# A fused attention and long-convolution kernel: both task lists in another sequence, evictions shared anew, and the last spectra's first two PSUM tiles in another pool

## The chip, the cores and the metric

The kernel runs on one core of one Trainium2 chip. The time is device microseconds of one execution, as the median of the runs. Five engines work side by side, each through its own list of instructions in order: PE (TensorE, matmuls; its weight loads are the rows named PEld), DVE (VectorE), ACT (ScalarE), POOL (GpSimd, here almost only DMA issues) and SP (SyncE, DMA issues). An engine waits on a semaphore when its next instruction needs another engine or a DMA, and everything behind that instruction on the same engine waits with it.

## The reference, cut to what matters

`S = L = 2048`, `D = 640`, 32 heads of 20, `N = 192` states. The output mixes a dilated local attention with a long convolution, by a gate per position:

```python
g = sigmoid((x * gate_w).sum(-1, keepdims=True))
# a: 8 keys per query, at distance 0, 2, ..., 14
qkv = x @ wqkv
attn = softmax(where(mask, einsum("bhsd,bhswd->bhsw", q, kg) * scale, -1e9))
a = einsum("bhsw,bhswd->bhsd", attn, vg) ... @ wo
# b: convolution of x with a kernel K made of 192 complex exponentials per channel
P = exp((dt * A)[:, :, None] * l)
K = einsum("dn,dnl,dn->dl", Cc, P, dt * Bc).real
y = irfft(rfft(x padded) * rfft(K padded))[:L] + x * Dskip
out = g * a + (1 - g) * y
```

Both branches read the same `A_x`.

## The kernel before

The work is cut into small tasks. A task has a name, an engine (or, for an eviction from PSUM, either of ACT and DVE), its dependencies, and buffers that it takes and gives back. The strings in `ORDER` hold two lists, `main` (1258 tasks) and `tail` (304): each number is the step to the next task's index in the list of tasks as they were made, and a `D` behind it puts an eviction on DVE, where it would else be ACT's. `Plan.order` reads the string, and `Plan.emit` writes the tasks out in that sequence and ties each instruction to the one before it on its engine. So the string sets the order of every engine, of the DMA queues of SP and POOL among them, and nothing reorders it later. No cost is computed when the kernel is built.

**Projections.** `late{n}` makes tile `n = 15*sc + 5*which + e`: quarter `sc` of the sequence (512 positions), `which` of q, k and v, and head group `e`. It is five matmuls of 128x512 (L281) from `bufA`, which holds the transposed x and `wqkv`, into one of two PSUM tiles named `tb`; `lev{n}` evicts it on ACT or DVE, q and k into the rings `qr` and `kr`, v into `prj`. The loads are issued before the list starts and stand in the same order in both kernels. On SP: `C_re`, `C_im`, the first quarter of x as a DMA transpose (L186), the q block of `wqkv` (L187), `A_im`, `A_re`, the k block, the v block, then quarters 1, 2 and 3 of x.

**Parameters.** Some thirty operations on 128x960 tiles on DVE and ACT (`wr`, `wi`, `tau`, `xl`, `ay`, `at`, and ten pieces `mk0` to `mk9`, tile `pc`) turn the state parameters into ten bf16 pieces, which SP stores (`sp0` to `sp9`, L615) and loads back in another layout (`L0` on SP and POOL, L726, and `L1` to `L9` on SP). On ACT stand among them the logarithm of `xl` (L650), its exponential into `ay` (L654), and `lnd` (L651); DVE's `ay` (L585) needs that exponential.

**Kernel generation.** Ten chunks. In each, `arg` tasks on PE (L761) put arguments into one of two PSUM tiles `ar` of two banks each; ACT takes Sin (L776) and Exp (L778) of them; DVE multiplies them (`pq`, L798 and L800); `kmm` on PE (L816) contracts them into `kps`; `fin` evicts. After chunk 4 half of the kernel is expanded: `near0`, `own0` and `other0`, a store to DRAM (`xst0S` on SP, L892 and L893, and `xst0G` on POOL, L890), and a load back as `kc` (`xld0S`, `xld0G`, L899). `f17` is the first matmul task that reads it (L1264).

**Attention.** Eight blocks of 256 positions: `prod` on DVE (L340), `lg` on PE (L346), the softmax (`max`, `neg`, `exp`, `sum`, `at`), the weights through DRAM on SP (`ast`, `asb`), `pv` on DVE (L409), `gat` on PE (L416), `oT`, the output projection `wo` on PE (L440), its eviction `ga`, and a store by SP (`gaS`, L461). V goes through DRAM on POOL: `lst{sc}2` stores a quarter of `prj` (L310), `vc{position}` loads a window of it (L334). The loads of x for the convolution (`rows`, tile `Usb`, L960) take `prj`'s memory, so the first of them waits for all four stores.

**Transforms.** `f1` and `fk` transform the kernel's two halves, `fu` transforms x; all three use `ar` tiles, and half of the tiles of `fk` use `tb`.

**Tail.** 64 tiles `fp` of four matmuls (L1031), evicted by `sp` tasks on ACT or DVE into spectra; DVE multiplies them (`ta`, `tc`, `Y`); `inv` on PE (L1092), `cp` evictions, `yp` (L1122), scaling and mixing, and the stores of the output. The `fp` tiles take turns in two PSUM pools of two tiles: pool 0 covers the banks that `kps`, `lg` and `tb` had before, pool 1 the banks of the two `ar` tiles. The first tile of a pool waits until the last user of its banks is done.

Of the kernel before, what the change touches and what calls it, by code (L numbers as in the profile page):

```python
# [13 lines left out]
F32 = mybir.dt.float32  # L14
# [26 lines left out]
def _attn_consts():  # L41
# [56 lines left out]
)}  # L98


# [1264 lines left out]
```

## Time and profile before

| | |
|---|---|
| median of 3 runs | 322.88 us (320.05 to 324.29) |
| the profiled execution's own time | 325.58 us |
| its span, first to last instruction | 323.8 us |
| mean granted TensorE clock | 0.966 |
| instructions | 11726 |
| DMA | 45.65 MB in 48697 packets, mean 141 GB/s |
| HBM | 28.25 MB read, 14.01 MB written |

The profiled execution's time is 1.8 us above its span, and 2.7 us above the median of the runs. In a busy line, the first number is microseconds in which the engine worked, then its share of the span and the number of instructions. In a row of the timeline stand the start, the time to the end of the last of the grouped instructions, engine, line, operation, output<-input, how many, and in brackets the idle time just before and what ended it. Neighbouring instructions of one engine overlap a little, so a step from start to start is a better price than a duration.

### The profile page before, as it was taken

Reading aid. Unit: us, or ns where it says so; the run is one execution under the profiler, and the core shown is the slowest. Engines: PE = TensorE matmul, PEld = TensorE weight load, DVE = VectorE, ACT = ScalarE, POOL = GpSimd, SP = SyncE. Lnnn points to the kernel's source line nnn. Section 1 sums busy time; section 2 is a strip of 40 time slices with the busy share of each in tenths; the row PEclk is TensorE's granted clock in tenths of the full one; section 3 lists DMA queues with packets and bytes.
Section 4 is the critical chain, followed back from the end, with each engine's and each line's share of the span. In section 5 each row is a group of like instructions: output and inputs, shape, how many; then the busy total and the mean of one; then the engine's idle time right before and its main releaser. Section 6 shows DMA issues by size and latency. Waiting matters only on the chain.

```text
span 323.8 us, 11726 instructions
## 1 busy us (share of the span) xinstructions
PE 280.7 (87%) x5126; PEld 167.5 (52%) x5126; DVE 289.4 (89%) x395; ACT 281.7 (87%) x422; POOL 55.9 (17%) x87
## 2 busy tenths in 40 slices
PE   0399999999999999999959988888999899997760
PEld 0046544445454555545535454447768676667640
DVE  1999989999999999998967999897998599998882
ACT  1489669999999999999968999799998799997891
POOL 8500073101100000302111302032010000000063
PEclk9999999999999999999998999599999999997995
DMA  8999127943050200558695675544480366873057
GB/s 212 340 221 286 66 61 189 207 116 113 7 124 8 67 5 33 115 103 281 205 237 128 148 167 103 117 134 95 167 304 27 89 211 228 191 146 62 2 134 194
DMA packets 48697, 45.65 MB, mean 141 GB/s; under 512 B 28590, under 2 KB 42482, under 8 KB 48646
## 3 DMA queue, kind: packets, MB, share of 16 engines
q1 hardware_dynamic: 42524, 27.82, 31.8%
q0 software_dynamic: 5216, 16.39, 20.8%
q8 instruction: 40, 0.66, 0.9%
q10 hardware_dynamic: 906, 0.69, 0.7%
q14 instruction: 11, 0.09, 0.1%
HBM read 28.25 MB, written 14.01 MB: 131 GB/s over the span
## 4 chain that ended last, share of the span: by engine, by line
PE 59%; ACT 22%; DVE 7%; DMA 5%; issue 4%; POOL 1%; SPq 0%; DVEq 0%; POOLq 0%; ACTq 0%
PE tb L281 18%; PE ar L761 8%; PE fp L1031 7%; PE tb L440 6%; ACT big L778 6%; PE kps L816 5%; ACT big L776 5%; PE bp L1264 4%; PE tb L416 4%; ACT bufA L468 2%; PE lg L346 2%; DMA bufA<-in_A_x_dram 2%; DMA bufA<-in_A_wqkv_dram 2%; PE cp L1092 2%; ACT bufA L776 2%
## 5 line engine op out<-in xcount | busy, mean ns | idle before, releaser
L281 PE MATMUL tb<-bufA 128*128 128x512 bf16 x300 | 77.3, 393 | 4.6 <-DMA bufA<-in_A_wqkv_dram 4.6
L776 ACT ACTIVATE big<-ar 128x740 bf16<-128x740 int16 (+1 forms) x72 | 56.4, 842 | 5.8 <-PE ar L761 5.5
L761 PE MATMUL ar<-Rarg,L 64*128 64x212 bf16 (+4 forms) x600 | 48.3, 254 | 5.5 <-ACT big L778 2.0
L778 ACT ACTIVATE big<-ar 128x848 bf16<-128x848 f32 x60 | 49.8, 906 | 1.0 <-PE ar L761 0.9
L281 PEld LDWEIGHTS <-bufA 128*128 128x128 bf16 x300 | 31.8, 122 | 35.5 <-issue 9.9
L340 DVE TENSOR_TENSOR prod<-qr,kr 128x2048 bf16<-128x2048 bf16 x40 | 48.0, 1219 | 2.0 <-PE lg L346 2.0
L409 DVE TENSOR_TENSOR pv<-vc,asb 128x2048 bf16<-128x2048 bf16 x40 | 47.5, 1219 | 0.5 <-PE tb L416 0.5
L761 PEld LDWEIGHTS <-L 64*128 64x128 bf16 x600 | 21.1, 95 | 37.5 <-issue 35.6
L798 DVE TENSOR_TENSOR pt<-big 128x1024 bf16<-128x1024 bf16 x48 | 32.7, 702 | 1.5 <-ACT big L776 0.7
L816 PE MATMUL kps<-qq,pt 128*32 128x21 bf16 (+1 forms) x2560 | 28.8, 175 | 5.9 <-issue 5.2
L816 PEld LDWEIGHTS <-pt 128*32 128x32 bf16 (+1 forms) x2560 | 23.5, 92 | 17.6 <-issue 15.4
L440 PE MATMUL tb<-wo_sb,oTm 128*128 128x320 bf16 x160 | 28.5, 315 | 0.1
L334 POOL DMA_DIRECT2D vc<-vS x16 | 11.6, 728 | 85.4 <-DVE pv L409 81.3
L468 ACT ACTIVATE sp_u<-fp 128x640 bf16<-128x640 f32 x30 | 22.5, 886 | 1.4 <-PE fp L1031 1.4
L468 ACT ACTIVATE sp_k<-fp 128x640 bf16<-128x640 f32 x31 | 23.0, 880 | 0.2 <-PE fp L1031 0.2
L416 PE MATMUL tb<-pv,ind 128*64 128x512 bf16 (+1 forms) x192 | 22.2, 350 | 0.2
L800 DVE TENSOR_TENSOR qq<-big 128x1344 bf16<-128x1344 bf16 x24 | 21.2, 885 | 0.0
L1031 PEld LDWEIGHTS <-PHI 128*128 128x128 bf16 x160 | 15.6, 97 | 8.5 <-issue 1.7
L468 ACT ACTIVATE big<-bp 128x1024 bf16<-128x1024 f32 x18 | 18.0, 1043 | 1.3 <-PE bp L1264 1.3
L440 PEld LDWEIGHTS <-oTm 128*128 128x128 bf16 x160 | 14.8, 101 | 8.0 <-issue 3.0
L157 ACT ACT_TABLE_LOAD x14 | 18.0, 1283 | 0.2
L1149 POOL DMA_DIRECT2D out_dram<-ot x14 | 7.8, 561 | 51.2 <-DVE ot L1131 50.4
(149 smaller groups left out, 488.7 us busy)
## 6 DMA issues: line engine op xcount, KB each, us to landing
vc<-vS POOLq DMA_DIRECT2D x16, 327.5 KB, 5.6
vS<-prj POOLq DMA_DIRECT2D x4, 640.0 KB, 5.2
gaS<-ga SPq DMA_DIRECT2D x8, 320.0 KB
Usb<-in_A_x_dram POOLq DMA_DIRECT2D x8, 320.0 KB, 5.0
gaF<-gaS SPq DMA_DIRECT2D x8, 320.0 KB
bufA<-in_A_wqkv_dram SPq DMA_DIRECT2D x3, 800.0 KB
Sprm<-pc SPq DMA_DIRECT2D x10, 240.0 KB
L<-Sprm SPq DMA_DIRECT2D x38, 60.0 KB
```

What stands on the lines that cost most here:

```text
L281: nc.tensor.matmul(ppf, self.wq[:, which, kt, e::5], self.xT[:, c0 // 1024, kt, c0 % 1024:c0 % 1024 + SC], start=(kt == 0), stop=(kt == NK ...
L340: nc.vector.tensor_tensor(b[e][:], self.qr[:, sc % NRB, e, :].unsqueeze(1).to_broadcast([128, W, C]), win(self.kr[:, sc % NRB, e, :], 0, W ...
L409: nc.vector.tensor_tensor(o, vw, b["asb"][:].unsqueeze(2).to_broadcast(sh), ALU.mult)
L416: nc.tensor.matmul(b["op", e][64 * a:64 * a + 64, 0:n, :], ind[:, 32:96], b["pv", e][:, w, a, 0:n, :], start=(w == 0), stop=(w == 3), skip ...
L440: nc.tensor.matmul(apf[:, :320], b["oT"][:, e, i * 128:(i + 1) * 128], wo_sb[:, e, hf * 320:(hf + 1) * 320], start=(e == 0), stop=(e == 4))
L468: nc.scalar.activation(o, i, ACT.Identity)
L761: nc.tensor.matmul(ar[:, g2, a0:a0 + ncol], L[rows, gv, sb, l0:l0 + 128], R[rows, c0:c0 + ncol], start=True, stop=True, tile_position=(64 ...
L776: nc.scalar.activation(d_[:, :, s0 * QW:s1 * QW], ar[:].bitcast(I16)[:, :, 0:2 * (s1 - s0) * QW:2], ACT.Sin, scale=SCL)
L778: nc.scalar.activation(dst[:, gp::2].rearrange("p g s n -> p g (s n)"), ar[:, :, 0:2 * EW], ACT.Exp)
L798: nc.vector.tensor_tensor(pt[:, :, k, :], gg[:, :, ::-1] if k else gg, e1, ALU.mult)
L816: nc.tensor.matmul(kps[32 * g:32 * g + 32, h ^ (g // 2), NM * ql:NM * ql + NM], pt[rows, k, v, :], qq[rows, k, v, :], start=(g not in star ...
L1031: nc.tensor.matmul(fp[:, fl % 2, 0:320].rearrange("p (c x) -> p c x", x=32), phis[fb][:, fl, kind, :], B[:, :, 2 * f1 + ri].rearrange("p c ...
```

## The change

Both strings of `ORDER` are replaced. The tasks, their dependencies and their buffers are the same; the sequence of both lists differs from the first task on, and some evictions change engine. In `main`, ACT evicts 48 of the 60 projection tiles where it evicted 45, 13 of 24 `oT` where it was 17, 21 of 32 `ga` where it was 20, 16 of 20 `fu` where it was 18, 9 of 15 `fk` where it was 8, and 8 of 10 `fin` where it was 6; DVE has the rest. In `tail`, ACT evicts 58 of the 64 `fp` tiles where it was 61, and 12 of the 20 `cp` tiles in both. ACT loads its function tables 14 times in both lists, at the same tasks. The one other edit turns the two pools of the `fp` tiles round:

```diff
 ORDER = {"main": (
-    "55 -48 49 -56 3 -2 3 7 -9 4 2 -3 7 -3 48 -44 -3 13 5 -14 2 -1 7 45 1 1 -17 1 1 -23 -14 8 -1 34 -25 26 1 19 1 1 -34 -29 "
+    "52 1 -52 2 -3 2 5 -1 6 -8 7 -3 46 -41 -8 127 1 1 -119 -6 1 18 -14 65 1 1 -34 -31 1 50 1 1 7 1 1 -23 1 -31 -7 39 13 1 1 "
...
-                    fp = spec[nm, ro, h] = q["ps"][q["nf"] // 2 % 2].tile([128, 2, 512], F32, name="fp")
+                    fp = spec[nm, ro, h] = q["ps"][1 - q["nf"] // 2 % 2].tile([128, 2, 512], F32, name="fp")
```

The first place is the start of PE's list. A row is an instruction with the semaphore that it waits on, the numbers behind a name tell tiles apart, and of the five matmuls of a tile the later ones are left out. Before, the first three projection tiles are `late1`, `late5` and `late0` (q, k and q of quarter 0):

```order
L281 LDWEIGHTS bufA_77 [waits DMAHW7_49]
L281 MATMUL tb_182<-bufA_77 128x512 [waits DMAHW3_49]
...
L281 LDWEIGHTS bufA_77 [waits DMAHW3_49]
L281 MATMUL tb_210<-bufA_77 128x512
...
L281 MATMUL tb_217<-bufA_77 128x512 [waits Activation_49]
```

Now they are `late0`, `late26` (v of quarter 1) and `late9` (k of quarter 0):

```order
L281 LDWEIGHTS bufA_77 [waits DMAHW7_49]
L281 MATMUL tb_182<-bufA_77 128x512 [waits DMAHW3_49]
...
L281 LDWEIGHTS bufA_77 [waits DMAHW4_49]
L281 MATMUL tb_201<-bufA_77 128x512 [waits DMAHW5_49]
...
L281 LDWEIGHTS bufA_77 [waits DMAHW3_49]
L281 MATMUL tb_213<-bufA_77 128x512 [waits Activation_49]
```

What moved: a tile of quarter 1 stands in the second place, and waits for two further loads, the v block of `wqkv` (DMAHW4) and quarter 1 of x (DMAHW5); before, the first tile of quarter 1 was PE's eleventh.

The second place is ACT's list at the same time; `qr`, `kr` and `prj` rows are evictions of those tiles, L650, L651 and L654 are the logarithm, `lnd` and the exponential of the parameters. Before:

```order
L594 ACTIVATE xl_149<-wr_142 128x960
L594 ACTIVATE ax_144<-wr_142 128x960
L594 ACTIVATE xa_148<-wi_143 128x960
L468 ACTIVATE qr_172<-tb_182 128x2x256
L650 ACTIVATE xl_149<-xl_149,bc0_152 128x960
L654 ACTIVATE ay_145<-xl_149 128x960
L651 ACTIVATE lnd_135<-dtb_133 128x5
L468 ACTIVATE kr_173<-tb_210 128x2x256
```

Now:

```order
L594 ACTIVATE xa_148<-wi_143 128x960
L594 ACTIVATE xl_149<-wr_142 128x960
L468 ACTIVATE qr_172<-tb_182 128x2x256
L594 ACTIVATE ax_144<-wr_142 128x960
L468 ACTIVATE prj_181<-tb_201 128x512
L651 ACTIVATE lnd_135<-dtb_133 128x5
L650 ACTIVATE xl_149<-xl_149,bc0_152 128x960
L468 ACTIVATE kr_173<-tb_213 128x2x256
L654 ACTIVATE ay_145<-xl_149 128x960
```

What moved: the evictions of `late26` and `late9` now stand ahead of the logarithm and of the exponential.

The third place is POOL's list around the expanded first half of the kernel (`xst0G` writes `Kx`, `xld0G` reads `kc`). Before, with the stores of quarters 2 and 3 of V (L310) on either side of it (the second reads like the first and is left out):

```order
L310 DMA vS_68<-prj_181 640x1x512
L890 DMA Kx_180<-X_3235 64x4x640
L899 DMA kc_3618<-Kx_180 128x2560
L334 DMA vc_3762<-vS_68 64x10x262 x2
...
L960 DMA Usb_4229<-in_A_x_dram 32x32x160 x2
```

Now, with the store of quarter 3 ahead of these rows, that of quarter 2 among them, and `vc1024` (the last row) behind the first load of `Usb`:

```order
L231 DMA omS_58<-om2_559 16x128
L890 DMA Kx_180<-X_3206 64x4x640
L899 DMA kc_3514<-Kx_180 128x2560
L310 DMA vS_68<-prj_181 640x1x512
L960 DMA Usb_3529<-in_A_x_dram 32x32x160
L334 DMA vc_3918<-vS_68 64x10x262 x2
```

What moved: the store of quarter 2 went from ahead of `xst0G` to behind `xld0G`, and the load of the fifth window of V behind it and behind a load of `Usb` that waits for that store. On SP, `gaS1` now stands ahead of `xst0S`; before, it stood behind it.

82 rows, old and new, of the table ORDER are left out of this document.

## The prediction

> **What bounds the kernel.** I read the page first: busy times, then the shares of the chain that ended last.
>
> ```profile
> span 323.8 us, 11726 instructions
> PE 280.7 (87%) x5126; PEld 167.5 (52%) x5126; DVE 289.4 (89%) x395; ACT 281.7 (87%) x422; POOL 55.9 (17%) x87
> PE 59%; ACT 22%; DVE 7%; DMA 5%; issue 4%; POOL 1%; SPq 0%; DVEq 0%; POOLq 0%; ACTq 0%
> ```
>
> Three engines are at 87 to 89% each, so no one engine is the bound, and a sequence can only win or lose waits. Where waits are left is read from the windows: the time, then busy time and count of PE, PEld, DVE, ACT and POOL, the granted clock, the DMA share and GB/s. The cuts are the first Sin, two spells of stalls, the end of `main` and the last spectra.
>
> ```profile
> 47.40:160.00 112.60, 110.62 (x2393) 56.50 (x2391) 110.09 (x153) 110.17 (x161) 12.50 (x19) 1.00 0.44 113
> 160.00:176.00 16.00, 12.09 (x283) 7.23 (x279) 11.77 (x17) 11.63 (x17) 3.92 (x5) 0.89 0.72 165
> 176.00:200.00 24.00, 21.22 (x571) 12.36 (x572) 23.19 (x30) 23.78 (x35) 6.02 (x8) 1.00 0.59 135
> 200.00:216.00 16.00, 13.35 (x288) 6.72 (x288) 14.28 (x16) 13.69 (x21) 2.83 (x5) 0.79 0.66 145
> 216.00:254.60 38.60, 35.94 (x534) 27.24 (x534) 33.86 (x50) 35.37 (x49) 5.41 (x10) 1.00 0.42 129
> 254.60:293.60 39.00, 36.58 (x258) 24.82 (x259) 35.86 (x51) 36.66 (x61) 0.46 (x2) 1.00 0.74 190
> ```
>
> From the first Sin to 160 us all three are at 98%: nothing lost at the start is made up there. From 160 to the end of `main` ACT idles 4.4 + 0.2 + 2.3 + 3.2 = 10.1 us; that is all that a better sequence could win back.
>
> **The start.** It is the one place where the change adds a wait that rows of before can price. The chain, the DMA packets in two windows (4.9 to 8.1 and 17.2 to 20.1 us), and then PE:
>
> ```profile
> 1.66 7.21 DMA bufA<-in_A_x_dram
> 8.89 6.80 DMA bufA<-in_A_wqkv_dram
> DMA packets 2955, 0.78 MB, mean 242 GB/s; under 512 B 2903, under 2 KB 2955, under 8 KB 2955
> DMA packets 2697, 0.74 MB, mean 256 GB/s; under 512 B 2633, under 2 KB 2697, under 8 KB 2697
> 11.82 2.33 PE L281 MATMUL tb<-bufA 128*128 128x512 bf16 x5 [2.99 <-DMA bufA<-in_A_wqkv_dram]
> 15.74 11.51 PE L281 MATMUL tb<-bufA 128*128 128x512 bf16 x45 [1.59 <-DMA bufA<-in_A_wqkv_dram]
> 17.86 0.15 PEld L281 LDWEIGHTS <-bufA 128*128 128x128 bf16 x1 [0.28 <-issue]
> 18.29 0.84 PEld L281 LDWEIGHTS <-bufA 128*128 128x128 bf16 x4 [0.28 <-issue]
> ```
>
> A quarter of x is 512 x 640 bf16, which is 2560 packets of 256 bytes. Quarter 0 fills the first of the two windows and has landed at 1.66 + 7.21 = 8.87, 0.8 us after the window's end. Quarter 1 fills the second, behind the weight blocks that SP issued ahead of it, so it lands at 20.1 + 0.8 = 20.9 us (20.1 at the earliest). Before, PE's first tile of quarter 1 came eleventh and found it there. Now it is second: PE does `late0` as before from 11.82, and then stands until 20.9 instead of 15.74, 5.2 us more, with `late9` and all that follows queued behind. `late26` takes 5 steps of 0.43 (from 17.86 to 18.29 the clock is still slow) and ends at 23.0.
>
> [...]
>
> What waits for PE at 23.0 are the parameters: ACT now has the evictions of `late26` and `late9` ahead of its logarithm and its exponential.
>
> ```profile
> 16.61 1.10 ACT L650 ACTIVATE xl<-xl,bc 128x960 f32<-128x960 f32 x1 [1.34 <-DVE xl L585]
> 17.74 1.00 ACT L654 ACTIVATE ay<-xl 128x960 f32<-128x960 f32 x1
> 18.65 0.19 ACT L651 ACTIVATE lnd<-dtb 128x5 f32<-128x5 bf16 x1
> 18.75 0.58 ACT L468 ACTIVATE kr<-tb 128x512 bf16<-128x512 f32 x1
> 21.02 1.15 DVE L585 TENSOR_TENSOR ay<-ay,ax 128x960 f32<-128x960 f32 x1
> 22.09 0.65 DVE L606 TENSOR_SCALAR x<-tau 128x960 f32<-128x960 f32 x1
> 22.66 1.15 DVE L585 TENSOR_TENSOR xa<-are,dtb 128x960 f32<-128x960 bf16 x1
> 38.39 1.15 DVE L622 TENSOR_TENSOR pc<-at,t 128x960 bf16<-128x960 f32 x1
> 41.67 0.70 SPq L726 DMA_DIRECT2D L<-Sprm  x2
> 42.18 1.42 POOL L726 DMA_DIRECT2D L<-Sprm  x2 [29.16 <-DMA L<-Sprm]
> L<-Sprm POOLq DMA_DIRECT2D x2, 60.0 KB, 2.6
> 47.00 0.53 PE L761 MATMUL ar<-Rarg,L 64*128 64x296 bf16 x8
> 47.41 2.42 ACT L776 ACTIVATE big<-ar 128x888 bf16<-128x888 int16 x3 [0.18 <-PE ar L761]
> ```
>
> From 23.0: eviction 0.58, `lnd` 0.19, logarithm 1.10, eviction 0.58, exponential 1.00, so 26.5, and only then DVE's `ay`, which stood at 21.02: 5.5 us late. DVE runs its list in order, so nothing covers this: ahead of `ay` the new list has one two-input and one single-input operation fewer, so DVE is there at 21.02 - 1.6 = 19.4 and stands for 7.1 us. Between `ay` and the last parameter piece the new list has one two-input operation (1.07 from 21.02 to 22.09) and one single-input one (0.57 from 22.09 to 22.66) more: 1.6 us. The last piece ends at 39.54 + 5.5 + 1.6 = 46.6 instead of 39.54. From there to `L0` landed it was 42.18 + 1.42 + 2.6 - 39.54 = 6.7 us, so the first `arg` can run at 53.3; it ran at 47.00. PE itself comes there at 47.00 + 5.2 + one more tile (5 steps of about 0.22) = 53.3. **+6.4 us** (bounds: 5.2, PE's pause alone, and 7.1, the delay of the pieces).
>
> That DVE no longer begins with `dtc`, which waits for ACT, gains nothing: it then waits longer at `ay`. What ACT has left at the first Sin is the same 150 Sin and Exp tasks and table loads and one eviction fewer of 92; I take 0, with up to -1.3 (4 `oT` and 2 `fu` fewer against 2 `fin`, a `lev`, a `ga` and a `fk` more).
>
> **The middle.** Everything else in `main` is a new interleaving on engines that were full to 160 us. POOL's and SP's moves (`vc0` ahead of `lst12`, the small `Dk` and constant loads later, `asb0` ahead of `ast1`, `asb2` behind `L4` to `L6`, `gaS0` behind `ast4`) are issues of under 3 us on queues that mostly wait, ahead of the DVE or ACT task that needs them; that lead is their cover, and if it is gone the task waits as in the first rival. I take 0, the value nearest to the 98% windows. Its bounds are the rows of the stalls after them:
>
> ```profile
> 144.77 0.39 SPq L892 DMA_DIRECT2D Kx<-X  x1
> 153.41 0.55 POOL L899 DMA_DIRECT2D kc<-Kx  x1 [5.79 <-DMA Kx<-X]
> 162.15 0.88 POOL L310 DMA_DIRECT2D vS<-prj  x1
> 168.31 0.21 PE L816 MATMUL kps<-qq,pt 64*32 64x21 bf16 x7 [3.14 <-issue]
> 171.38 1.58 POOL L960 DMA_DIRECT2D Usb<-in_A_x_dram  x2 [8.35 <-DMA vS<-prj]
> 204.53 0.25 PE L816 MATMUL kps<-qq,pt 64*32 64x21 bf16 x9 [1.49 <-issue]
> ```
>
> Below: the pauses of PE at 168.31 and 204.53, both inside a run of `kps` and with no releaser, cost ACT 4.4 + 2.3 = 6.7 us. Above: a new wait like POOL's or PE's here, 3 us.
>
> **The tail.** The seam, ACT's two groups of evictions, and the chain:
>
> ```profile
> 254.58 1.25 PE L1031 MATMUL fp<-big,PHI 128*128 128x320 bf16 x8 [0.83 <-ACT ga L449]
> L468 ACT ACTIVATE sp_u<-fp 128x640 bf16<-128x640 f32 x30 | 22.5, 886 | 1.4 <-PE fp L1031 1.4
> L468 ACT ACTIVATE sp_k<-fp 128x640 bf16<-128x640 f32 x31 | 23.0, 880 | 0.2 <-PE fp L1031 0.2
> 254.58 22.84 PE fp L1031 x164
> ```
>
> The first `fp` waited 0.83 for the last `ga`, whose PSUM tile lies in pool 0. It now takes the banks of `ar`, which are free two PE tasks earlier: -0.7 (0 to -0.83), hidden if ACT is late there. In the spectra, 3 of 61 evictions of about 0.6 (39.00 us of window for 61) leave ACT: up to -1.8; but PE makes a tile in 22.84/41 = 0.557, 64 of them 35.7, against 37, so -1.3 at most, and DVE takes three more within an idle time of 3.1: -0.7. The rest keeps its counts: 0.
>
> **Sum:** +6.4 - 0.7 - 0.7 = +5.0 on a span of 323.8. That execution's own time, 325.58, lies 2.7 above the median; I put the difference on the median: 322.88 + 5.0 = 328.
>
> **Rivals.**
>
> *The middle adds a wait* (slower). On SP `xst0S` now stands behind `gaS1`, so the store of the expanded half leaves later, and `kc` behind it; before, store to load took from 144.77 to 153.41. POOL then stores quarter 2 of V behind `xld0G`, the first load of `Usb` waits for it (8.35 us at 171.38), and `vc1024` stands behind that. It decides if PE reaches `f17`, or DVE `pv40`, before these land. Against it: before, all of this had slack. Price: about PE's worst stall, 3: 331.
>
> *The pauses at 168 and 204 do not come back* (not slower): -6.7, so 321.3. For it: no instruction asked for them, and they fell where DMA was at 0.72 and 0.66 of its time; in another order the same runs of `kps` meet other transfers. Against it: the new list puts its V store and `Usb` loads in the same stretch. It decides if no PE pause over 1 us is left between 160 and 216.
> [...]
>
> *The start costs nothing* (not slower): if quarter 1 lands with the v block, or PE's delay is hidden, the sum is -1.4: 321.5. Against it: packets of quarter 1 run to 20.1, and DVE, ACT and PE all wait in the same chain.
>
> **Chances.** Forecast 0.48 (its own range 325 to 331), the added wait 0.22, no pauses 0.20, no cost at the start 0.10. The range reaches to the other cases: 319.5 to 333.5. A change under 2% is about what a measurement of this kernel cannot tell from none: 316.4 and 329.3 are the marks. Slower by over 2%: a third of the forecast's and nearly all of the added wait, 0.36. Faster by over 2% needs two of the gains together: 0.07. Within 2%: 0.57.
>
> **What would show it.** Right: in the new profile PE waits at its sixth matmul for `bufA<-in_A_x_dram` to about 21; DVE idles some 7 us before `ay`; the first Sin starts near 54; `fp` starts without a wait for `ga`; ACT's spectra end sooner after the first `fp`. Wrong: a first Sin before 50, or a `main` that is longer from the first Sin to the first `fp` than the 207.2 us of before by more than 3 us, or shorter by more than 6.

## The result, and the profile after

| | before | changed |
|---|---|---|
| median, first comparison | 323.5 us (4 runs, 320.05 to 324.29) | 332.24 us (4 runs, 331.25 to 333.32) |
| ratio, with its 95% interval | | 1.0295 (1.023 to 1.036) |
| the same, timed again | 326.01 us (17 runs, 321.04 to 330.59) | 330.78 us (6 runs), 1.020 (1.014 to 1.026) |
| a third time, on another chip | 324.98 us (18 runs, 322.07 to 331.01) | 331.62 us (5 runs), 1.027 (1.025 to 1.030) |
| profiled execution: time, span | 325.58, 323.8 us | 331.25, 329.5 us |

The changed kernel is slower, by 4.8 to 8.7 us from median to median. All ratios here are of the faster executions of each kernel (within 1.5% of its fastest), so where a kernel's runs spread widely, as before's do, they differ from the ratio of the medians, by up to 1.6% here. One thing stands out before any trace is opened: the runs of before spread over 1.3% in the first comparison and nearly 3% in the others, those of the changed kernel over 0.5 to 1%.

The start first: the timeline of the changed kernel, with PE's first two tiles, the weight loads behind the pause, ACT's and DVE's rows of the parameters, and the first Sin.

```profile
11.70 2.33 PE L281 MATMUL tb<-bufA 128*128 128x512 bf16 x5 [3.21 <-DMA bufA<-in_A_wqkv_dram]
21.29 11.69 PE L281 MATMUL tb<-bufA 128*128 128x512 bf16 x44 [7.26 <-DMA bufA<-in_A_x_dram]
24.23 0.15 PEld L281 LDWEIGHTS <-bufA 128*128 128x128 bf16 x1 [0.27 <-issue]
24.61 2.49 PEld L281 LDWEIGHTS <-bufA 128*128 128x128 bf16 x12 [0.23 <-issue]
23.62 0.60 ACT L468 ACTIVATE prj<-tb 128x512 bf16<-128x512 f32 x1 [8.07 <-PE tb L281]
25.73 0.99 ACT L654 ACTIVATE ay<-xl 128x960 f32<-128x960 f32 x1
26.76 1.16 DVE L585 TENSOR_TENSOR ay<-ay,ax 128x960 f32<-128x960 f32 x1 [8.49 <-ACT ay L654]
45.76 1.15 DVE L622 TENSOR_TENSOR pc<-t,t 128x960 bf16<-128x960 f32 x1
53.93 0.36 PE L761 MATMUL ar<-Rarg,L 64*128 64x296 bf16 x4
54.78 3.07 ACT L776 ACTIVATE big<-ar 128x888 bf16<-128x888 int16 x4
```

PE's second tile waits for `bufA<-in_A_x_dram` and starts at 21.29. ACT waits 8.07 us for that tile, DVE 8.49 us for ACT, and the first Sin starts at 54.78 where it started at 47.41. The rest of the span is read from three windows, first Sin to first `fp`, to the first inverse matmul, and to the end: before, then changed (time, then busy time and count of PE, PEld, DVE, ACT and POOL, granted clock, DMA share, GB/s).

```profile
47.41:254.58 207.17, 193.19 (x4059) 110.03 (x4056) 193.19 (x262) 194.63 (x278) 30.65 (x46) 0.98 0.49 125
254.58:293.55 38.97, 36.55 (x258) 24.79 (x257) 35.81 (x51) 36.66 (x61) 0.48 (x2) 1.00 0.74 190
293.55:323.80 30.25, 16.83 (x576) 15.38 (x576) 21.22 (x35) 20.63 (x34) 7.77 (x14) 0.80 0.36 92
```

```profile
54.78:260.74 205.96, 188.47 (x4033) 109.10 (x4054) 192.39 (x261) 195.26 (x277) 33.71 (x52) 1.00 0.51 127
260.74:299.72 38.98, 36.43 (x256) 24.75 (x255) 37.93 (x54) 34.93 (x58) 0.21 (x1) 1.00 0.72 172
299.72:329.50 29.78, 16.91 (x576) 15.35 (x576) 21.23 (x35) 20.63 (x34) 7.72 (x14) 0.81 0.36 93
```

(In the first of the changed windows 21 matmul records are missing, 4033 against 4054 weight loads, so its PE time reads too low.) The start costs 54.78 - 47.41 = +7.4, the middle -1.2, the spectra 0.0, the end -0.5: together the 5.7 us between the two spans. In the spectra three evictions did go from ACT to DVE (instructions in the window: ACT 61 to 58, DVE 51 to 54): ACT is idle 4.1 us there instead of 2.3, DVE 1.0 instead of 3.2, and the length is the same to 0.01 us.

Two executions are few where one kernel spreads by 3%, so the same four stretches stand here for three profiles of each (before: the first, the one with the pools turned, and the repetition below; changed: the first and the two repetitions below):

| us | before's list | changed | difference of the means |
|---|---|---|---|
| to the first Sin | 47.41, 48.67, 50.00 | 54.78, 55.97, 56.21 | +7.0 |
| to the first `fp` | 207.17, 201.77, 209.43 | 205.96, 204.72, 205.19 | -0.8 |
| to the first inverse matmul | 38.97, 38.96, 38.95 | 38.98, 39.00, 38.99 | 0.0 |
| to the end | 30.25, 29.40, 29.72 | 29.78, 30.21, 29.41 | 0.0 |

The first Sin of one list moves by 2.6 us, and PE's rows tell why. In the changed kernel's rows above, the weight loads behind the pause stand about 0.43 us apart until 24.61, and 0.21 us from there on: PE begins with steps twice as long. Behind its wait for k, before's list has 6, 13 and 18 such slow steps in the three profiles (the last of them in two spells, and in the second, 34.12 to 37.52, the granted clock reads 0.50); the changed list has 8, 12 and 12 behind its pause. At 0.43 - 0.22 = 0.21 us each, the 12 steps between 6 and 18 are worth 2.5 us.

### The profile page after: what moved, and what is told of

It is laid out like the page before. It is cut to its first block, busy times and chain, and to the rows that moved or that the text cites. A ratio compares the mean times of both kernels' runs of the same rounds, so it can differ in the third digit from the quotient of the medians.

```text
span 329.5 us, 11700 instructions
## 1 busy us (share of the span) xinstructions
PE 277.4 (84%) x5102; PEld 167.2 (51%) x5126; DVE 290.9 (88%) x397; ACT 281.5 (85%) x420; POOL 55.7 (17%) x87
## 5 line engine op out<-in xcount | busy, mean ns | idle before, releaser
L281 PE MATMUL tb<-bufA 128*128 128x512 bf16 x276 | 73.7, 394 | 12.8 <-DMA bufA<-in_A_x_dram 7.3
L761 PE MATMUL ar<-Rarg,L 64*128 64x212 bf16 (+4 forms) x600 | 49.0, 251 | 8.7 <-ACT big L776 3.5
L816 PE MATMUL kps<-qq,pt 128*32 128x21 bf16 (+1 forms) x2560 | 27.9, 175 | 1.9 <-issue 1.5
L440 PE MATMUL tb<-wo_sb,oTm 128*128 128x320 bf16 x160 | 26.5, 300 | 0.6 <-DVE ga L451 0.6
L468 ACT ACTIVATE sp_k<-fp 128x640 bf16<-128x640 f32 x30 | 22.2, 926 | 1.3 <-PE fp L1031 1.3
L468 ACT ACTIVATE sp_u<-fp 128x640 bf16<-128x640 f32 x28 | 21.2, 941 | 1.9 <-PE fp L1031 1.9
L468 ACT ACTIVATE prj<-tb 128x512 bf16<-128x512 f32 x18 | 11.0, 613 | 12.4 <-PE tb L281 12.2
L468 ACT ACTIVATE big<-bp 128x1024 bf16<-128x1024 f32 x16 | 16.3, 1037 | 2.2 <-PE bp L1264 1.9
```

The costliest lines, as they stand in the source:

```text
L281: nc.tensor.matmul(ppf, self.wq[:, which, kt, e::5], self.xT[:, c0 // 1024, kt, c0 % 1024:c0 % 1024 + SC], start=(kt == 0), stop=(kt == NK ...
L440: nc.tensor.matmul(apf[:, :320], b["oT"][:, e, i * 128:(i + 1) * 128], wo_sb[:, e, hf * 320:(hf + 1) * 320], start=(e == 0), stop=(e == 4))
L468: nc.scalar.activation(o, i, ACT.Identity)
L761: nc.tensor.matmul(ar[:, g2, a0:a0 + ncol], L[rows, gv, sb, l0:l0 + 128], R[rows, c0:c0 + ncol], start=True, stop=True, tile_position=(64 ...
L816: nc.tensor.matmul(kps[32 * g:32 * g + 32, h ^ (g // 2), NM * ql:NM * ql + NM], pt[rows, k, v, :], qq[rows, k, v, :], start=(g not in star ...
```

## Experiments on the start

Each run is timed against before on its own chip; the interval behind a ratio is at 95%. First, `late26` was taken back out of the second place (names of tasks, in the order of the list):

```diff
 changed kernel, main:
 ... lev0 xl act_ax
-late26 late26b lev26
 lnd near_x1 tau near_s1 act_xl late9 late9b lev9 ...
 ... lg00 lg01 sp3 prod02 sp8 sp4
+late26 late26b lev26
 late22 act_at late22b lev22 ...
```

> The changed kernel with the tile late26 and its eviction moved behind late7, to the 10th place on PE and in front of the first other tile of quarter 1; nothing else differs. Theory 'start': the pause for quarter 1 carries the first Sin from 47.4 to 54.8 us, and this alone is the loss. Then PE waits at its sixth matmul only for the k block to about 15.7, the first Sin comes at 48 to 49, and the time falls from 332.2 to 325 to 326, within 1% of before. Rival 'middle': the new interleaving behind the first Sin costs the time, and PE and DVE make up the late start there; then the first Sin comes early but the time stays at 329 or above.

327.0 us (6 runs) against 326.34 (17 runs), ratio 1.017 (1.008 to 1.026). PE and the first Sin, in the timeline of this kernel:

```profile
16.68 5.50 PE L281 MATMUL tb<-bufA 128*128 128x512 bf16 x15 [2.15 <-DMA bufA<-in_A_wqkv_dram]
50.60 3.07 ACT L776 ACTIVATE big<-ar 128x888 bf16<-128x888 int16 x4
```

The long pause is gone and the first Sin comes 4.2 us sooner than in the changed kernel, though not at 48 to 49. The time leaves it open how much of the loss is gone: by the medians all but 0.7 us, by the ratio 1.7% are left, and the interval holds 2%. The opposite edit put `late26`, alone, into the list of before:

```diff
 kernel before, main:
 ... tau mk0 near_s1
+late26 late26b lev26
 act_xl act_ay lnd stt_xl late5 late5b lev5 ...
```

> The kernel before with late26 alone moved up to PE's second place, its eviction ahead of the logarithm of the parameters on ACT; nothing else differs. Theory 'start': PE stands until quarter 1 lands at about 21, DVE's ay follows at about 26 instead of 21.0, the first Sin comes at 53 to 54, and the time goes from 323.5 to 329 to 331. Rival 'middle': the delay is taken up behind the first Sin and the time stays under 326.

330.25 us (6 runs) against 326.34, ratio 1.028 (1.019 to 1.037), and in its timeline:

```profile
21.73 0.58 PE L281 MATMUL tb<-bufA 128*128 128x512 bf16 x1 [6.97 <-DMA bufA<-in_A_x_dram]
55.12 2.42 ACT L776 ACTIVATE big<-ar 128x888 bf16<-128x888 int16 x3 [0.18 <-PE ar L761]
```

One moved tile brings the whole late start into a list that is otherwise that of before: theory "start" holds. From the first Sin to the first `fp` this kernel takes 206.3 us, within before's 201.77 to 209.43, so the middle doesn't make it up. The loss in time is 3.9 us by the medians; the ratio is clear of 1, but not of 2%. Which way the pause takes to the first Sin was the next question: the logarithm and the exponential were put ahead of the late evictions.

```diff
 changed kernel, main:
 ... late26 late26b
-lev26 lnd near_x1 tau near_s1 act_xl late9 late9b lev9 xa act_ay ay
+near_x1 tau near_s1 lnd act_xl act_ay lev26 late9 late9b lev9 xa ay
 late5 late5b lev5 ...
```

> The changed kernel with late26 still second on PE, but on ACT lnd, the logarithm and the exponential of the parameters ahead of the evictions of late26 and late9, so that DVE's ay no longer waits for PE. It tells the two ways apart in which the pause delays the first Sin. If the parameters are the way (ay from 26.8 back to about 20, the last piece from 46.9 to about 41), the first Sin comes at about 50 and the time is 328 to 329. If PE's own list is the way (it comes to its first arg 5.5 us late whatever the parameters do), the first Sin stays at 53.5 to 54.5 and the time at 331 to 332.

330.38 us (6 runs) against 326.34, ratio 1.029 (1.023 to 1.034). The timeline of DVE, ACT and PE:

```profile
18.50 1.15 DVE L585 TENSOR_TENSOR ay<-ay,ax 128x960 f32<-128x960 f32 x1
27.58 1.23 DVE L340 TENSOR_TENSOR prod<-qr,kr 128x2048 bf16<-128x2048 bf16 x1 [7.35 <-ACT kr L468]
46.25 1.15 DVE L622 TENSOR_TENSOR pc<-t,t 128x960 bf16<-128x960 f32 x1
46.45 3.40 PE L281 MATMUL tb<-bufA 128*128 128x512 bf16 x14 [0.24 <-ACT qr L468]
55.27 3.07 ACT L776 ACTIVATE big<-ar 128x888 bf16<-128x888 int16 x4
```

`ay` runs at 18.50 instead of 26.76, and nothing comes of it. DVE now stands 7.35 us at its first `prod`, which needs a q and a k tile of PE, and the last parameter piece and the first Sin are as late as before this edit. So the edit did not free the parameters: the exponential was only one of two places where DVE met the delay. What settles the way is PE. From the end of its pause at 21.11 to its first `arg` at 54.42, PE has one wait of over 0.2 us, the 0.24 at 46.45 for ACT, and in the three profiles of the changed kernel it likewise has this one alone. PE doesn't stand for the parameters there: its own list, late by the pause, sets the first Sin.

If PE's list sets it, work for PE in the wait for the k block should help before too. `late0` (q) went ahead of `late5` (k), once with its eviction only, and once with the evictions placed so that PE's fourth tile need not wait for them:

```diff
 kernel before, main, first version:
 ... act_xl act_ay lnd stt_xl
-late5 late5b lev5 late0 late0b lev0
+late0 late0b lev0 late5 late5b lev5
 second version:
 ... mk0 near_s1
+late0 late0b lev0 late5 late5b
 act_xl
+lev5
 act_ay lnd stt_xl
-late5 late5b lev5 late0 late0b lev0
```

> The kernel before with late0 (a second q tile) ahead of late5 (the first k tile) and their evictions likewise. PE then has work while the k block is on its way, so the wait of 1.6 us at 15.7 goes. If PE's own list sets the first Sin, as the run with the exponential first suggests, the first Sin comes 0.8 to 1.6 us sooner (46 to 46.6), and the time falls by about as much: 0.3 to 0.5%. If the parameters set it, nothing moves.

> The kernel before with late0 second on PE as in the earlier run, and now its eviction right behind that of late1 on ACT (ahead of the logarithm) and that of late5 between the logarithm and the exponential, so that PE does not wait 2.0 us for ACT at its fourth tile. DVE's ay has some 1.5 us to spare there. If PE's list sets the first Sin, it comes about 1 us sooner than in the kernel before (profiles 47.4, 48.7, 50.0), at 46.5 to 48.5, and the time is 1 to 2 us (0.3 to 0.6%) under that of before, at the limit of what these runs can tell. If the parameters set it, the time is that of before.

322.95 us (12 runs) against 326.01, ratio 0.993 (0.988 to 0.999); and 325.13 us (12 runs) against 324.98, ratio 1.003 (0.999 to 1.008). The first Sin came at 48.73 and 49.59, within the 47.41 to 50.00 of before. PE's rows of the second version:

```profile
12.09 4.24 PE L281 MATMUL tb<-bufA 128*128 128x512 bf16 x10 [2.83 <-DMA bufA<-in_A_wqkv_dram]
16.63 3.43 PE L281 MATMUL tb<-bufA 128*128 128x512 bf16 x15 [0.30 <-DMA bufA<-in_A_wqkv_dram]
22.29 2.26 PE L281 MATMUL tb<-bufA 128*128 128x512 bf16 x6 [2.23 <-ACT qr L468]
```

The wait for k shrank from 1.6 to 0.3 us, and PE gave it back three tiles later, for an eviction that ACT held up. This was a miss: the interval of the first version ends just under 1, that of the second holds 1, so no gain is proven.

## Experiments on the middle and on the tail

The lists were cut behind the second Sin and joined crosswise: the start of before with the changed rest (run twice), and the changed start with the old rest, beside the changed kernel on one chip.

```diff
 start of before, changed rest (tail and pools changed):
+the first 160 tasks of main in the sequence of before
 all other tasks of main in the changed sequence
 changed start, rest of before (tail and pools of before):
+the tasks of main to lev24 in the changed sequence
 all other tasks of main in the sequence of before
```

> The changed kernel with its main list begun as before: the first 160 tasks in the sequence of before (to the second Sin), then all others in the changed sequence; the tail list is the changed one. Theory 'start': the whole loss sits ahead of the first Sin; then that comes at 47.4 to 50.0 as in the three profiles of before, and the time is that of before within 1%, or 1 to 2 us under it since PE pauses less in this order. Rival 'middle': the new interleaving costs as well; then the first Sin is early and the time still lies 3 us or more above before.

> The reverse of the run that begins as before: the kernel before with its main list begun as in the change (to the task ahead of the third chunk piece's arguments), then all others in the sequence of before, tail and pools of before. Theory 'start': the whole loss is here: first Sin at 54.5 to 56, and the time 5 to 8 us above before, no less than the changed kernel's. Rival 'middle': part of the loss stays away with the old middle; then the time lies 3 us or more under the changed kernel's.

> The changed kernel on the chip of the other three, as the corner with both new: 4 to 9 us above before; first Sin 54.5 to 56.0.

> The changed kernel with the start of before once more, as the corner with the old start and the new rest. Theory 'start': within 1% of before and 4 to 7 us under the changed kernel. Rival 'middle': closer to the changed kernel than to before.

| main | median | ratio |
|---|---|---|
| before | 324.98 us (18 runs) | |
| old start, changed rest | 326.83 (6 runs) | 1.014 (1.010 to 1.017) |
| the same, earlier | 327.15 (8 runs, before 325.03) | 1.010 (1.005 to 1.014) |
| changed kernel | 331.62 (5 runs) | 1.027 (1.025 to 1.030) |
| changed start, old rest | 339.58 (8 runs) | 1.039 (1.035 to 1.042) |

By the medians the old start wins back 331.62 - 326.83 = 4.8 of the 6.6 us; by the ratios it is half of the loss (1.014 against 1.027). What remains need not be the middle's. The row of the first 22 us behind the first Sin, in before and in the joined list:

```profile
47.40:70.00 22.60, 22.00 (x341) 10.07 (x337) 21.98 (x31) 22.23 (x32) 5.07 (x8) 1.00 0.78 176
```

```profile
48.29:70.00 21.71, 19.73 (x162) 7.83 (x159) 17.27 (x25) 18.73 (x28) 4.14 (x7) 0.92 0.53 118
```

ACT idles 0.4 us there in before and 3.0 in the joined list, DVE 0.6 and 4.4. In the changed kernel itself ACT idles 0.3 us in the first 22.6 us behind its first Sin, so the waits belong to the join: a start hands the rest a certain set of finished tiles, and the changed rest was made for another set. The other crossing shows it more strongly: it is 8 us slower than the changed kernel itself, so it tells what a bad join costs, not what the start does. If a join only costs, the corners bound the start from below by 4.8 us and put the rest (middle, tail and pools together) at some 2 us at most, both by the medians. Two of the expectations failed here: the old start was to come within 1% of before (1.014 in the second run), and the changed start was to cost 5 to 8 us (it cost 14.6).

The swap of the PSUM pools was made alone:

```diff
-                    fp = spec[nm, ro, h] = q["ps"][q["nf"] // 2 % 2].tile([128, 2, 512], F32, name="fp")
+                    fp = spec[nm, ro, h] = q["ps"][1 - q["nf"] // 2 % 2].tile([128, 2, 512], F32, name="fp")
```

> The kernel before with the two PSUM pools of the fp tiles turned round, and both lists as before. By the prediction's term for the seam the first fp starts at once instead of after 0.83 us for the last ga: 0.0 to 0.8 us faster, so 322.7 to 323.5. The rival: ACT is behind at that place, the first tiles wait for its last evictions in the other banks, and the time is the same or up to 1 us longer. The list of main is that of before, instruction for instruction: if the two pauses of PE of 3.14 and 1.49 us at 165 and 203 belong to the list, they stand here again at the same matmuls; if they belong to one execution, they do not.

324.36 us (12 runs) against 326.34, ratio 1.007 (1.001 to 1.013). ACT, DVE and PE at the seam in this kernel's timeline, and ACT and DVE in that of before:

```profile
249.78 0.52 ACT L449 ACTIVATE ga<-tb,g_sb 128x320 bf16<-128x320 f32 x1
249.07 1.23 DVE L470 CAST bufA<-bp 128x1024 bf16<-128x1024 f32 x1 [0.44 <-PE bp L1264]
250.44 1.25 PE L1031 MATMUL fp<-big,PHI 128*128 128x320 bf16 x8 [0.92 <-ACT ga L449]
```

```profile
254.01 0.52 ACT L449 ACTIVATE ga<-tb,g_sb 128x320 bf16<-128x320 f32 x1
253.30 1.23 DVE L470 CAST bufA<-bp 128x1024 bf16<-128x1024 f32 x1 [0.44 <-PE bp L1264]
```

The other banks come free with DVE's last `bp`, at 249.07 + 1.23 = 250.30, and the last `ga` ends at 249.78 + 0.52 = 250.30. The first `fp` waits for one as long as for the other, and the swap moves nothing. The rows of before say the same: both evictions end at 254.53. In the changed list the first `fp` waits 1.41 us, for ACT's last eviction from just these banks.

## Experiments on the pauses of PE

The pauses of before with no releaser were a rival of the forecast, so before was profiled again:

> The kernel before, unchanged, for a second profile. If the pauses at 165 and 203 belong to places in the list, they stand at the same two matmuls with other lengths, and the time differs from the first profile's 325.58 by about the difference of their lengths; if they belonged to that one execution, they are gone.

329.82 us, one run. The time was to differ from the first profile's by the pauses' lengths and did not: they add up to nearly the same, and the span is 4.2 us longer, 2.6 of them ahead of the first Sin. Here are the rows of PE at the same two tasks, in this execution and the one with the pools turned, and at the first of them in the two with `late0` second; the first profile's stand in the prediction.

```profile
172.40 0.23 PE L816 MATMUL kps<-qq,pt 64*32 64x21 bf16 x7 [3.23 <-issue]
209.06 0.25 PE L816 MATMUL kps<-qq,pt 64*32 64x21 bf16 x9 [1.30 <-issue]
```

```profile
166.60 0.21 PE L816 MATMUL kps<-qq,pt 64*32 64x21 bf16 x7 [0.31 <-issue]
201.63 0.23 PE L816 MATMUL kps<-qq,pt 64*32 64x21 bf16 x9 [1.62 <-issue]
```

```profile
171.23 0.23 PE L816 MATMUL kps<-qq,pt 64*32 64x21 bf16 x7 [4.54 <-issue]
```

```profile
169.93 0.23 PE L816 MATMUL kps<-qq,pt 64*32 64x21 bf16 x7 [2.32 <-issue]
```

In the first task the pause stands always 7 matmuls from the end, in the second 9, and at the first place it is 0.31 to 4.54 us long. Counted through PE's list (every matmul and every weight load), the two places are the instructions 5560 and 7096 of before, 1536 or 6 times 256 apart. So a shift of the list should move them. The gate's small matmul was repeated, into the same words, at a time when PE waits for its weights:

```diff
+        for _ in range(41):
-        nc.tensor.matmul(lt[:, 0, 0:5], g5[:], at_.ident[0:5, 0:5], start=True, stop=True)
+            nc.tensor.matmul(lt[:, 0, 0:5], g5[:], at_.ident[0:5, 0:5], start=True, stop=True)
```

> The kernel before with the gate's small matmul (L567) written 41 times instead of once, into the same PSUM words: 80 PE instructions more, at a time when PE waits for the weights in any case (8.3 to 11.8 us). The order is that of before. Theory 'fetch': PE pauses in kps where the next 256 instructions have not been fetched, and these places lie at fixed counts of instructions; then the pause that stood after 57 of 64 matmuls of a kps task (3.14, 2.04 and 0.31 us in three traces) is not there any more, and any pause of PE in kps with no releaser lies 80 instructions (40 matmuls) earlier in the list, or in other runs of kps. Theory 'order': the pause belongs to the transfers that this order puts there; then it stays after the 57th matmul, 0.3 to 3 us long. Time: that of before within 1%, up to 4 us less if the new places are outside dense runs of kps.

> The kernel before with the gate's small matmul (L567) 25 times instead of once: 48 PE instructions more in time that PE waits anyhow. Theory 'fetch': PE pauses where 256 instructions in a row run out faster than the next 256 come in while the DMA engines are busy. From the start times of the PE instructions in the first profile, with the pauses taken out, the shortest block between 150 and 235 us lasts 2.7 us as the list stands (it ends at the pause of 165 us) and 3.7 us with a shift of 48. Then no pause of over 1 us is left between 150 and 235 us, the median falls by 2 to 5 us under that of before (0.6 to 1.5%), and the runs spread less. Rival: the pauses only move, as with the shift of 80, and the time stays within 1% of before with the same spread.

> The kernel before with the same small matmul 73 times: 144 PE instructions more. It is the opposite test of theory 'fetch': with this shift the blocks of 256 instructions between 150 and 235 us that last least take 1.3 us (it ends near 191 us in the first profile's time), 2.3 and 2.7 us. Then a pause of 3 us or more stands there, two or three of over 1 us in all, and the time lies 2 to 6 us above before. If PE's pauses have nothing to do with counts of instructions, the time is that of before but for up to 1 us at the start.

The second of these has `range(25)`, the third `range(73)`. Times: 332.16 us (6 runs) against 326.01, ratio 1.015 (1.007 to 1.023); 325.54 (12 runs) against 325.03, 0.999 (0.994 to 1.003); 332.69 (6 runs) against 325.03, 1.022 (1.018 to 1.026). PE's pauses of over 1 us with no releaser behind 160 us, with the shift of 80, of 48, and of 144:

```profile
175.04 0.72 PE L440 MATMUL tb<-wo_sb,oTm 128*128 128x320 bf16 x2 [3.55 <-issue]
```

```profile
175.87 0.72 PE L440 MATMUL tb<-wo_sb,oTm 128*128 128x320 bf16 x4 [2.10 <-issue]
226.80 0.46 PE L817 MATMUL kps<-qq,pt 128*32 128x21 bf16 x40 [1.18 <-issue]
```

```profile
172.33 0.37 PE L817 MATMUL kps<-qq,pt 64*32 64x21 bf16 x27 [2.44 <-issue]
200.52 0.26 PE L762 MATMUL ar<-Rarg,L 64*128 64x212 bf16 x1 [1.73 <-issue]
229.48 0.29 PE L817 MATMUL kps<-qq,pt 64*32 64x21 bf16 x16 [1.91 <-issue]
```

No pause stands 7 matmuls from the end of that `kps` task any more; with the shifts of 80 and 48 the long one falls on a `wo` matmul, with no releaser either. The pauses in these rows stand at the instructions 5816, 6840 and 8116 of the shifted lists, multiples of 256 away from 5560 to within 4. All 52 such pauses of over 0.25 us behind the first 40 us, in the 17 profiles of this case, stand at such counts, to within 4. So they belong to counts of PE instructions, and the order decides which work stands there. With a poor shift (144) the same order is about 2% slower: the three pauses foreseen came, though the longest is 2.44 us and not 3, and the loss is 7.7 us by the medians, over the 2 to 6 foreseen. My remedy failed: the shift of 48 left a pause of 2.10 us at the end of a block that took about 4 us by the start times of its instructions, longer than the one that the expectation feared, so the length of a block alone doesn't foretell the pause.

What ends a pause stands among the DMA packets. A row of the page of before:

```profile
q8 instruction: 40, 0.66, 0.9%
```

These are 40 packets of 16,384 bytes, and PE has 10252 matmuls and weight loads, 10252 / 40 = 256 to a packet. The five executions of the first place, by length of the pause, in us:

| | last weight load ends | packet | PE goes on |
|---|---|---|---|
| pools turned | 166.2 | 163.57 to 165.19 | 166.60 |
| `late0` second, second version | 167.5 | 166.87 to 168.33 | 169.93 |
| before, first profile | 165.1 | 165.28 to 166.80 | 168.31 |
| before, repetition | 169.1 | 169.47 to 170.88 | 172.40 |
| `late0` second, first version | 166.6 | 168.52 to 169.67 | 171.23 |

PE goes on 1.4 to 1.6 us behind the end of the packet, however long it stood. The same holds for all 40 pauses of over 0.5 us behind the first 40 us in the 17 profiles: they end 1.3 to 1.8 us behind a packet's end. By these times I take it that PE stands there for its own instructions, and that a pause is as long as their packet is late.

Last, the changed kernel was profiled and timed once more.

> The changed kernel once more, beside the three below. Theory 'start' says that the difference of the medians is the 7.4 us of the first Sin and little else: 6 to 9 us above before, first Sin at 54.5 to 55.0, from there to the first fp 203 to 206, and from the first fp to the first inverse matmul 39.0 as in all kernels so far. Rival 'pauses': how far the two medians lie apart hangs on how long PE pauses within runs of kps in each execution; then the runs of before spread by 3% or more, those of this kernel by 1%, and the difference of the medians changes by several us between chips.

330.78 us (6 runs, 328.45 to 331.86), 4.8 us above before by the medians where 6 to 9 were foreseen. First Sin at 55.97, then 204.72 to the first `fp`. Its longest pause of PE with no releaser behind 160 us is 0.87; in the first profile of the changed kernel they were these:

```profile
194.86 0.52 PE L816 MATMUL kps<-qq,pt 64*32 64x21 bf16 x48 [0.47 <-issue]
199.41 0.43 PE L761 MATMUL ar<-Rarg,L 64*128 64x212 bf16 x5 [1.57 <-issue]
226.25 0.35 PE L816 MATMUL kps<-qq,pt 64*32 64x21 bf16 x29 [1.07 <-issue]
```

Together 3.1 us, where the first profile of before has 3.14 + 1.49 and the second 3.23 + 1.30.

The granted clock falls around these pauses too. In before's first profile it reads 0.5 from 168.6 to 172.0, behind the first pause, and from 202.7 to 209.6, where the second pause follows three short waits for ACT. In none of the three profiles of the changed kernel does it fall between the first Sin and the first `fp`. The stretch between those two, in us, with what would be left of it without the pauses of over 0.25 us and without half of the time at clock 0.5 outside of them:

| | stretch | pauses | clock at 0.5 | left |
|---|---|---|---|---|
| before, first | 207.2 | 5.2 | 8.7 | 197.6 |
| pools turned | 201.8 | 1.9 | 3.4 | 198.1 |
| before, repetition | 209.4 | 5.2 | 11.0 | 198.8 |
| changed, first | 206.0 | 3.1 | 0 | 202.8 |
| changed, again | 204.7 | 0.9 | 0 | 203.9 |
| changed, third | 205.2 | 1.8 | 0 | 203.4 |

The last column is an estimate: it takes every pause at its full length and the slow clock at half its time. By it the new interleaving costs about 5 us in waits, and the pauses and the slow clock that it is spared are worth about 6. Of the other profiles, those with before's order behind the first Sin leave 197.4 to 201.6 (but for the bad join, 202.3), those with the changed order 201.0 to 204.1, so these sizes are good to a few us. Both theories had a part: the start makes the kernel slower by 7, and how far the medians lie apart follows the spread of before.

## Why the prediction was right or wrong

The time, 332.24 us, lies in the range and 4.2 us above the forecast of 328. A change within 2% was called the likeliest, and the ratio is 1.0295.

- **Quarter 1 lands at 20.9.** Right: 21.29, after a wait of 7.26 us.
- **The slow steps behind the pause.** The prediction reads `late26`'s steps of 0.43 us as a clock that is still slow. The rows show the steps: after the pause of 7.3 us, eight matmuls at steps of about 0.43 in the first profile of the changed kernel (21.29 to 24.61) and twelve in the second (21.69 to 26.73). The records of the granted clock begin only at the end of these steps, at 18.43 us in before and 24.54 in the changed kernel, so they don't show it for them. The sum has no term for more slow steps behind a longer pause, and rightly: before's list has 6, 13 and 18 behind a wait of 1.6 to 2.0 us, so the longer pause adds nothing that shows.
- **The first Sin +6.4.** The right mechanism: +7.4 from profile to profile, +7.0 over three of each. The working gave two ways of equal length, through the parameters and through PE's own list (both make 53.3 - 47.00 = +6.3, where the sum took +6.4). The traces show that PE's holds: it has no wait of over 0.24 us between its pause and its first `arg`, at 53.93. Against the other profiles of before the anchor was also an early mark: 47.41 is the earliest of three.
- **The seam -0.7.** Failed: both groups of banks come free at the same moment, in the profile of before already, and the swap alone changes nothing.
- **The spectra -0.7.** Failed: the time per tile is PE's, so what ACT was spared became idle time. The prediction had PE's step in hand (0.557 us, 35.7 for 64 tiles) and still counted a part of the gap to 37 as ACT's.
- **The middle 0.** Right in the number, -0.8 over three profiles of each, and by luck: by the estimate above, about +5 of new waits met about -6 of pauses and slow clock that did not come back. These are two of the rivals, and each was priced alone. The added wait did not come where the first rival looked for it: PE's longest wait for a DMA behind 160 us is 0.17, for `kc`. The pauses stand at other work and are shorter. Nor was the clock in the sum: the prediction priced the pauses by ACT's idle time, 6.7 us.

The step that failed is **the sum and where it was put**: "+6.4 - 0.7 - 0.7 = +5.0", set on the median by taking off the 2.7 us that the profiled execution of before lay above it. The 2.7 is the larger failure. It was taken for a property of the kernel, and it belonged to that execution: the changed kernel's profile lies 1.0 us below its own median (331.25 against 332.24), so the forecast lost 2.7 + 1.0 = 3.7 us here. What the runs show in its place are pauses, stretches of slow clock and slow first steps that change from one execution of before's list to the next: the three spans lie between 318.8 and 328.1 us. The sum itself was short by 0.7 us from profile to profile (+5.0 against +5.7). There the two credits of 0.7 measured 0 and the start 1.0 more than forecast, while -1.2 in the middle and -0.5 at the end, both put at 0, happened to make up for most of it. Without the credits the same start gives 322.88 + 6.4 = 329.3, the prediction's own mark for slower by over 2%.

In the first comparison the runs of before lay between 320.05 and 324.29, and the loss reads as 8.7; in the second and third they lay between 321 and 331, and it reads as 4.8 and 6.6.

What stays open: which waits of the changed middle make up the estimate's 5 us; what delays the packet of instructions in one execution and not in another; and the changed list without the swap of the pools, which was not tried.

## What to carry to other kernels

Here three engines were busy for 87 to 89% of the span, and one tile in PE's second place, whose input landed at 21.3 us, made PE wait 7.3 us and the first Sin come 7.0 us later, however little else depended on it; before moving a tile forward, look up when its load lands. Three evictions taken from ACT, which didn't set the step of the spectra, won nothing (38.97 and 38.98 us): price an eviction by the engine that paces the tiles. And profile a kernel that spreads by some per cent (three spans of before: 318.8 to 328.1 us) more than once before the difference to another is put down to the change, or one profile's excess over the median to the kernel.

## What the hardware showed that was not expected

PE paused with no releaser at fixed counts of its instructions: all 52 such pauses of over 0.25 us behind the first 40 us, in the 17 profiles, stand at multiples of 256 from one another to within 4, and at one and the same place the pause took 0.31 to 4.54 us. PE went on 1.3 to 1.8 us behind the end of a 16,384-byte packet of instructions, and around the two long pauses of before's first profile the granted clock read 0.5 for 3.4 and 6.8 us. Repeating a small matmul 72 times more, in time that PE spent waiting, moved those places and made the kernel about 2% slower (ratio 1.022). The first Sin of an unchanged list came at 47.41, 48.67 and 50.00, with 6, 13 and 18 of PE's steps ahead of it at 0.43 us instead of 0.21.
